# Top-k attention and two expert layers on one core: tiles regrouped over the last expert stages, conversions begun earlier, a pair's transposes put together

## The chip, the core and the metric

The kernel runs on one core of a Trainium2 chip. A core has TensorE (PE: matrix products, with a separate row, PEld, for its weight loads), VectorE (DVE), ScalarE (ACT), GpSimd (POOL) and SyncE (SP, which here only issues DMAs). Each engine takes its own instructions strictly in the order in which the program holds them. The metric is the device time of one execution in microseconds (us).

## The reference

Inputs: q, k, v of 2 batches x 8 heads x 576 rows x 64; 1152 tokens of 512 features leave the attention. What is computed, cut to its core:

```
scores = q k^T / 8;  kth = 32nd largest of each row;  keep scores >= kth
x   = softmax(kept scores) v                       # 1152 x 512
out = sum over 4 experts e of p[:, e] * (relu(x w1[e]) w2[e])      # hidden 1024
y   = max(out m1, out m2, out m3) m_out            # hidden 768
```

Everything is float32. The four weights of the last line (m1, m2, m3, m_out) arrive as 64-bit floats and are narrowed to 32 bits on the core.

## The kernel before

**Work items.** The 1152 tokens are 9 tiles of 128. The attention of one tile and one pair of heads is a "pair"; there are 36 pairs, numbered 0 to 35 in the order of `pairs`. For a pair and its two heads (j = 0, 1) the kernel computes scores (L419, L424, PE), copies them (L431, ACT), finds the 32 largest by four rounds of MAX8 and three of MATCH_REPLACE8 (L444, L446, DVE), masks and takes the exponential (L465 to L467 on ACT, or L458 on ACT and L472 on DVE), transposes the result (L490 and L495, PE; five transposes for j = 1 and the tail, four for j = 0), copies the transposes out (L493, L498, ACT), multiplies by v (L532, L535, PE, into `psv`), transposes the reciprocal of the sum (L518, `psr`), scales (L542, DVE) and splits the result into a high and a low part, `xh` (L555, ACT) and `xl` (L556, POOL).

**Slots.** `attention()` puts every step of pair n into a numbered slot, counted from 8n; dictionaries such as BOTH and LOOSE hold the offsets. `two(s, f, lag)` issues f in slot s and what f returns (mostly the copy out of PSUM) lag slots later. BOTH holds for pairs 8, 9, 10, 12, 13, 14; LOOSE for pairs 15 to 35; pair 11 has its own (THIRD), as have pairs 0 to 7. So in BOTH the transposes of j = 0 stand in slot 13, those of j = 1 and the tail in 14, their copies in 15 and 16; in LOOSE (trans=10, with the late mask of j = 0) the same. The product with v is in slot 17.

**Expert stages.** `STAGES` lists which tiles pass through which expert halves together. There are 9 stages, 0 to 8; even ones run the first 4 halves of the experts' hidden width, odd ones the last 4, so each tile is in one even and one odd stage. Before: [0], [0,1], [1,2], [2,3], [3,4], [4,5], [5], [6,7,8], [6,7,8]. A stage uses 16 weight blocks of 128x1024: 8 for the first layer ("a") and 8 for the second ("b"). In a stage of two or three tiles a product is done as three fast products of high and low parts (`product`, L681 to L683): 24 per first-layer block, with 128 columns per tile, and 6 of 512 columns per second-layer block and tile. Stages of one tile (`WHOLE`: 0 and 6) multiply plain float32 (L802: 8 per first-layer block, L843: 2 per second-layer block; each is recorded as two) and need no split weights. Elsewhere each block is split by `w_split_to`: a copy to the high part `whi` (L272, ACT) and the low part `wlo` (L278), in two halves on POOL, from stage LATE = 7 on every other block in one piece on DVE. `weight()` has blocks split up to W_AHEAD = 4 beyond the one in use.

**Who sets the order.** PE's expert work (`products`) is a generator. After each slot the main loop advances it until PE's estimated time has caught up with DVE's (`clock`), so expert matmuls fill PE between attention steps. A stage starts only when the attention of its newest tile is done.

**Conversions.** The 48 quarter blocks of the 64-bit weights go through `to_float32`: two ACT steps (L239, L240), three on DVE (L242, L244, L246), one on POOL (L249), and a DMA out (L254), spread over the slots. One starts every W_STEP = 2 slots from slot W_FROM = 306; their first loads (L223) are issued 6 slots before. The last attention steps are near slot 303.

Of the kernel before, what the change touches and what calls it, by code (L numbers as in the profile page):

```python
# [30 lines left out]
LATE = 7  # L31
ON_POOL = ((0, 1), (0, 1, 4))
W_AHEAD = 4
WIDE, W_FROM, W_STEP = 4, 306, 2
ON_ACT = (range(2, 36), (2, 5, 6, 8, 9, 10, 12, 13, 14))
STEEP = 2.0 ** 100
MASK_LATE = 2
# [3 lines left out]
TIGHT = dict(stag=3, new=1, scores=-7, at=(10, 11), guard=11, rec=11, spread=12, pv=12, turn=12, norm=13, split=13, last=14, lag=0, lag_s=1, sum=0, late=1)  # L41
SECOND = dict(TIGHT, norm=14, split=14, last=15)
THIRD = dict(stag=4, new=1, scores=-4, at=(11, 12), guard=12, rec=13, spread=13, pv=14, turn=14, norm=15, split=15, last=16, lag=0, lag_s=2, sum=0)
BOTH = dict(stag=4, new=1, scores=-4, at=(13, 14), pv=17, rec=15, lag=2, sum=0, late=1)
LOOSE = dict(stag=4, new=1, scores=-4, trans=10, pv=17, rec=15, lag=2, sum=0)

EARLY = 7

# [12 lines left out]
def kernel(  # L61
# [24 lines left out]
    NTILE = NT // P  # L86
# [7 lines left out]
    def batches(t):  # L94
        return (0, 1) if t == MIXED else (0 if t < MIXED else 1,)
# [2 lines left out]
    def place(t):  # L98
        return (t - 1) % RING

    STAGES = [[0]] + [[t - 1, t] for t in range(1, NTILE - 3)] + [[NTILE - 4]] + [[NTILE - 3, NTILE - 2, NTILE - 1]] * 2
    STAGES = [sorted(x, key=place) for x in STAGES]
    HALVES = [range(E) if not n % 2 else range(E, 2 * E) for n in range(len(STAGES))]
    WHOLE = [n for n, x in enumerate(STAGES) if len(x) == 1]
    FIRST_IN = {t: min(n for n, x in enumerate(STAGES) if t in x) for t in range(NTILE)}
    LAST_IN = {t: max(n for n, x in enumerate(STAGES) if t in x) for t in range(NTILE)}
    assert all(set(x for n in range(len(STAGES)) if t in STAGES[n] for x in HALVES[n]) == set(range(2 * E)) for t in range(NTILE))

# [3 lines left out]
    at = ctx.enter_context(tc.tile_pool(name="at", bufs=2))  # L112
# [445 lines left out]
    def attention():  # L558

        NP = len(pairs)  # L560
        prs = {}
        later, between = {}, {}

        def options(n):
            return TIGHT if n == HP - 1 else SECOND if n == 2 * HP - 1 else MIDDLE if n in (HP - 2, 2 * HP - 3, 2 * HP - 2) else FIRST if n < 2 * HP else THIRD if n == 3 * HP - 1 else BOTH if n in ON_ACT[1] else LOOSE

        def at_slot(s, f, *a):
            later.setdefault(s, []).append((f, a))


        first_use = {}
        for n, (c, hp, t) in enumerate(pairs):
            for b in batches(t):
                if ("v", b, hp) not in first_use:
                    first_use["v", b, hp] = n
                    at_slot(8 * n + (options(n)["pv"] - 7 if b and hp else 0), load_v, b, hp)
                if t >= FULL:
                    first_use.setdefault(("k", b, hp), n)
            if t >= FULL:
                first_use.setdefault(("q", c, hp), n)  # L580
            elif n:
                o = options(max(0, n - 2))
                at_slot(max(8 * n + options(n)["scores"] - LOAD_FULL, 8 * (n - 2) + o["scores"] + o["stag"] + 1), load_full, n)
        free = {"k": -99, "q": -99}
        for key, n in first_use.items():
            if key[0] == "v":
                continue
            s0 = 8 * n
            load, split = (load_k, split_k) if key[0] == "k" else (load_q, split_q)
            at = max(s0 + options(n)["scores"] - (SPLIT_K if key[0] == "k" else SPLIT_Q), free[key[0]] + 2)  # L590
            if key[0] == "k" and key[1] and key[2]:

                at = max(at, 8 * pairs.index((MIXED, key[2] - 1, MIXED)) + options(n)["scores"] + options(n)["stag"] + (1 if key[2] == HP - 1 else 4))
            at_slot(max(at - LOAD, free[key[0]] + 1), load, *key[1:])
            at_slot(at, split, *key[1:])
            free[key[0]] = at
        for n, (c, hp, t) in enumerate(pairs):
            s0 = 8 * n
            prs[n] = Pair(n)
            pr = prs[n]  # L600
            o = options(n)

            def two(s, f, *a, lag=o["lag"]):
                at_slot(s, lambda: at_slot(s + lag, f(*a)))
            for j in range(2):
                b0 = s0 + o["stag"] * j
                two(b0 + o["scores"], pr.scores, j, lag=o.get("lag_s", o["lag"]))
                for i in range(7):
                    if o["new"]:
                        later.setdefault(b0 + i, []).insert(0, (pr.topk, (j, i)))  # L610
                    else:
                        at_slot(b0 + i, pr.topk, j, i)
                at_slot(b0 + 2, pr.negate, j)
                at_slot(b0 + 5, pr.exp, j)
                late = o.get("late", MASK_LATE) * pr.on_act[j]
                two(b0 + 7 + late, pr.mask, j, lag=o["sum"] if n < EARLY else 3)
                two(s0 + o["at"][j] if "at" in o else b0 + o["trans"] + late + (late > 0), pr.trans_p, j)
            two(s0 + o["at"][1] if "at" in o else s0 + o["stag"] + o["trans"], pr.trans_p, 2)
            at_slot(s0 + o.get("guard", o["rec"] - 1), pr.guard)
            at_slot(s0 + o["rec"], pr.recip)  # L620
            at_slot(s0 + o.get("spread", o["rec"] + 1), pr.spread)
            at_slot(s0 + o["pv"], pr.pv)
            two(s0 + o.get("turn", o["rec"] + 2), pr.trans_r)
            end = max(o["pv"], o["rec"] + 2) + o["lag"]
            if "norm" in o:
                between.setdefault(s0 + o["norm"], []).append((pr.norm, ()))
            else:
                at_slot(s0 + end + 1, pr.norm)
            two(s0 + o.get("split", end + 2), pr.split_x)
        last = {}  # L630
        for n, p in enumerate(pairs):
            o = options(n)
            last[p[0:2]] = 8 * n + o.get("last", max(o["pv"], o["rec"] + 2) + 2 * o["lag"] + 2)
        for n in range(len(alone)):
            at_slot(ALONE_FROM + ALONE_STEP * n, load_alone, n + 1)
        end = max(last.values()) + 1
        s = min(later)
        while s <= end:
            todo = later.pop(s, [])
            i = 0  # L640
            while i < len(todo):
                f, a = todo[i]
                f(*a)
                todo[i + 1:i + 1] = between.pop(s, [])
                todo += later.pop(s, [])
                i += 1
            yield s, [c for c in last if last[c] + (READY if c[1] == HP - 2 else 0) == s]
            s += 1

        while narrowed[0] < WIDE * len(wide):  # L650
            clock["dve"] += PAUSE
            yield s, []
            s += 1


    lag = []
# [335 lines left out]
    for s, done in attention():  # L992
        if s == W_FROM - 6:
            for i in range(AHEAD_S):
                wide_load(i)
        if s >= W_FROM + W_STEP * conv and conv < WIDE * len(wide):
            converting.append(to_float32(conv))
            conv += 1
        for x in list(converting):
            if next(x, 0) == 0:  # L1000
                converting.remove(x)
        split_waiting()
        while any((x.c, x.hp) in done for x in waiting):
            assert advance()
            clock["goal"] = max(clock["goal"], clock["pe"])
            split_waiting()
        x_ready.update(done)
        clock["goal"] += (clock["dve"] - before) * SHARE[min(phase[0], len(SHARE) - 1)]
        before = clock["dve"]
        while clock["pe"] < clock["goal"]:  # L1010
            if not advance():
                clock["pe"] = clock["goal"]
                break
# [67 lines left out]
```

## Time and profile before

| | |
|---|---|
| median of 3 runs | 756.3 us (754.99 to 757.06) |
| the profiled execution | 755.31 us, its span 753.5 us |
| PE / DVE / ACT / POOL busy, share of the span | 97% / 80% / 66% / 61% |
| granted TensorE clock, mean | 0.998 |
| chain that ended last | PE 81%, ACT 8%, DVE 7% |

PE's busy share counts matmuls from start to a modelled end; they overlap, so the distance from one start to the next says what a matmul costs PE. What an engine waited for stands in brackets behind the instruction that waited. Pair 35's last attention step on PE (`psr`) begins at 446.04 us; before that, expert stages 0 to 6 and the attention share PE; after it come the rest of stage 6, stages 7 and 8, and the last layer.

### The profile page before, as it was taken

How to read it: one execution, taken by the hardware profiler on the slowest of the kernel's cores; microseconds unless marked ns; L12 is line 12 of the kernel's file. 1: busy time of each engine (PE TensorE's matmuls, PEld its weight loads, DVE VectorE, ACT ScalarE, POOL GpSimd, SP SyncE). 2: the span in 40 equal slices, each digit the busy share in tenths (PEclk: the TensorE clock that was granted, in tenths of full speed). 3: DMA queues.
4: the chain of work that ended last, by engine and by line, in shares of the span. 5: the costliest groups of instructions: out<-in, count | busy, mean ns of one | idle time of the engine just before them, and what ended most of it. 6: DMA issues, size and time to landing. Idle time of an engine off the chain costs nothing.

```text
span 753.5 us, 13557 instructions
## 1 busy us (share of the span) xinstructions
PE 728.9 (97%) x4678; PEld 643.6 (85%) x4678; DVE 604.8 (80%) x1160; ACT 495.1 (66%) x1127; POOL 457.7 (61%) x401
## 2 busy tenths in 40 slices
PE   6899998999999999999999999999999999999998
PEld 3586787878999998899988867999888899998996
DVE  6999987989999899999999958999999644233331
ACT  4668888889887887797796765666555533442531
POOL 2514777669979796787874316678677733442520
PEclk9999999999999999999999999999999999999999
DMA  7584554534646463534532769888688451443501
GB/s 221 180 269 153 160 179 156 151 100 134 212 129 196 124 195 110 181 120 149 158 121 90 251 216 352 248 263 284 219 266 267 142 187 69 154 168 104 190 1 43
DMA packets 56484, 130.14 MB, mean 173 GB/s; under 512 B 9760, under 2 KB 23328, under 8 KB 56416
## 3 DMA queue, kind: packets, MB, share of 16 engines
q1 hardware_dynamic: 48064, 120.69, 50.9%
q10 hardware_dynamic: 8352, 8.59, 3.2%
q8 instruction: 37, 0.61, 0.3%
q14 instruction: 31, 0.25, 0.1%
HBM read 120.60 MB, written 8.65 MB: 172 GB/s over the span
## 4 chain that ended last, share of the span: by engine, by line
PE 81%; ACT 8%; DVE 7%; issue 2%; POOL 1%; DMA 0%; ACTq 0%; POOLq 0%; DVEq 0%
PE ps L681 18%; PE ps L682 18%; PE ps L683 18%; PE psv L535 4%; PE pss L424 3%; DVE m L444 3%; PE psp L490 3%; DVE work L446 3%; ACT whi L272 2%; PE ps L843 2%; PE ps L802 2%; PE pso L682 2%; PE pso L681 2%; PE psa L766 2%; PE pso L683 2%
## 5 line engine op out<-in xcount | busy, mean ns | idle before, releaser
L278 POOL TENSOR_TENSOR wlo<-raw,whi 128x512 fp32r<-128x512 f32 x228 | 303.5, 1360 | 118.9 <-ACT whi L272 116.5
L272 ACT ACTIVATE whi<-raw 128x1024 fp32r<-128x1024 f32 x148 | 152.6, 1056 | 34.0 <-POOL narrow L249 16.4
L681 PE MATMUL ps<-xl,whi 128*128 128x256 f32 (+1 forms) x520 | 160.7, 309 | 0.1
L682 PE MATMUL ps<-xh,whi 128*128 128x256 f32 (+1 forms) x520 | 156.6, 301 | 0.0
L683 PE MATMUL ps<-xh,wlo 128*128 128x256 f32 (+1 forms) x520 | 156.5, 301 | 0.0
L444 DVE MAX8 m<-work 128x8 f32<-128x576 f32 x216 | 155.2, 745 | 0.1
L446 DVE MATCH_REPLACE8 work<-m,work 128x576 f32<-128x576 f32 x144 | 106.7, 741 | 0.0
L681 PEld LDWEIGHTS ps<-xl,whi 128*128 128x128 f32 x520 | 98.7, 190 | 1.5 <-POOL xl L556 0.3
L278 DVE TENSOR_TENSOR wlo<-raw,whi 128x1024 fp32r<-128x1024 f32 x34 | 53.3, 1567 | 57.3 <-ACT whi L272 45.1
L682 PEld LDWEIGHTS ps<-xh,whi 128*128 128x128 f32 x520 | 97.9, 188 | 1.2 <-issue 0.7
L683 PEld LDWEIGHTS ps<-xh,wlo 128*128 128x128 f32 x520 | 97.7, 188 | 0.0
L249 POOL TENSOR_TENSOR narrow<-narrow,raw 128x256 int32<-128x256 int32 x48 | 44.5, 927 | 40.1 <-DVE narrow L246 12.2
L681 PE MATMUL ps<-wlo,h 128*128 128x512 f32 x160 | 66.0, 413 | 0.6 <-POOL wlo L278 0.6
L683 PE MATMUL ps<-whi,h 128*128 128x512 f32 x160 | 63.2, 395 | 0.9 <-POOL h L818 0.9
L682 PE MATMUL ps<-whi,h 128*128 128x512 f32 x160 | 62.9, 393 | 0.0
L431 ACT ACTIVATE s<-pss 128x288 f32<-128x288 f32 x144 | 51.4, 401 | 12.6 <-PE pss L419 11.2
L444 DVE MAX8 m<-s 128x8 f32<-128x576 f32 x72 | 53.9, 748 | 4.5 <-ACT s L431 4.5
L446 DVE MATCH_REPLACE8 work<-m,s 128x576 f32<-128x576 f32 x72 | 53.4, 741 | 0.0
L493 ACT ACTIVATE pt<-psp 128x512 f32<-128x512 f32 x72 | 42.7, 594 | 16.2 <-PE psp L490 16.1
L683 PE MATMUL ps<-x2h,wlo 128*128 128x384 f32 x144 | 48.7, 338 | 0.0
L681 PE MATMUL ps<-x2l,whi 128*128 128x384 f32 x144 | 48.7, 338 | 0.0
L682 PE MATMUL ps<-x2h,whi 128*128 128x384 f32 x144 | 48.6, 337 | 0.0
(118 smaller groups left out, 1602.4 us busy)
## 6 DMA issues: line engine op xcount, KB each, us to landing
raw<-in_w_dram SPq DMA_DIRECT2D x112, 512.0 KB, 4.3
raw<-narrow SPq DMA_DIRECT2D x36, 512.0 KB, 3.9
whole<-in_w_dram SPq DMA_DIRECT2D x30, 512.0 KB, 5.5
raw<-in_m_dram SPq DMA_DIRECT2D x36, 256.0 KB, 4.8
narrow<-narrow ACTq DMA_DIRECT2D x48, 128.0 KB, 4.3
kraw<-in_k_dram SPq DMA_DIRECT2D x16, 288.0 KB, 4.3
qraw<-in_q_dram SPq DMA_DIRECT2D x48, 64.0 KB, 3.9
raw<-in_mo_dram SPq DMA_DIRECT2D x12, 256.0 KB, 4.1
```

What stands on the lines that cost most here:

```text
L249: nc.gpsimd.tensor_tensor(out=out.bitcast(I32), in0=out.bitcast(I32), in1=last, op=ALU.add)
L272: nc.scalar.activation(out=hi, in_=raw, func=AF.Copy)
L278: on.tensor_tensor(out=lo[:, x], in0=raw[:, x], in1=hi[:, x].bitcast(F32), op=ALU.subtract)
L424: nc.tensor.matmul(ps[:, 0:SH], lhsT=l, rhs=r, start=i == 0, stop=i == len(mm) - 1)
L431: nc.scalar.activation(out=s[:, h, :], in_=halves[h][:, 0:SH], func=AF.Copy)
L444: nc.vector.max(m[:, 8 * r:8 * r + 8], src)
L446: nc.vector.match_replace(out=self.w[j], in_to_replace=m[:, 8 * r:8 * r + 8], in_values=src, imm_value=NEG)
L493: return lambda: [nc.scalar.activation(out=d, in_=ps.rearrange("p (r n) -> p r n", r=NR), func=AF.Copy), self.did.add(("pt", part))]
L535: nc.tensor.matmul(ps[j * D:(j + 1) * D, cols], lhsT=vs[:, j * NR + r, :], rhs=self.pt[j][:, r, cols], start=False, stop=r == NR - 1)
L681: nc.tensor.matmul(ps, lhsT=lh, rhs=rl, start=first, stop=False)
L682: nc.tensor.matmul(ps, lhsT=lh, rhs=rh, start=False, stop=False)
L683: nc.tensor.matmul(ps, lhsT=ll, rhs=rh, start=False, stop=last)
```

## The change

Four settings and one argument:

```diff
-WIDE, W_FROM, W_STEP = 4, 306, 2
+WIDE, W_FROM, W_STEP = 4, 298, 2
-BOTH = dict(stag=4, new=1, scores=-4, at=(13, 14), pv=17, rec=15, lag=2, sum=0, late=1)
-LOOSE = dict(stag=4, new=1, scores=-4, trans=10, pv=17, rec=15, lag=2, sum=0)
+BOTH = dict(stag=4, new=1, scores=-4, at=(14, 14), pv=17, rec=15, lag=2, lag_t=1, sum=0, late=1)
+LOOSE = dict(stag=4, new=1, scores=-4, at=(14, 14), pv=17, rec=15, lag=2, sum=0)
-    STAGES = [[0]] + [[t - 1, t] for t in range(1, NTILE - 3)] + [[NTILE - 4]] + [[NTILE - 3, NTILE - 2, NTILE - 1]] * 2
+    STAGES = [[0]] + [[t - 1, t] for t in range(1, NTILE - 3)] + [[NTILE - 4, NTILE - 3], [NTILE - 3, NTILE - 2, NTILE - 1], [NTILE - 2, NTILE - 1]]
-                two(s0 + o["at"][j] if "at" in o else b0 + o["trans"] + late + (late > 0), pr.trans_p, j)
-            two(s0 + o["at"][1] if "at" in o else s0 + o["stag"] + o["trans"], pr.trans_p, 2)
+                two(s0 + o["at"][j] if "at" in o else b0 + o["trans"] + late + (late > 0), pr.trans_p, j, lag=o.get("lag_t", o["lag"]))
+            two(s0 + o["at"][1] if "at" in o else s0 + o["stag"] + o["trans"], pr.trans_p, 2, lag=o.get("lag_t", o["lag"]))
```

The stages after are [0], [0,1], ..., [4,5], [5,6], [6,7,8], [7,8]: stage 6 has two tiles and split weights instead of one tile and whole weights, stage 8 two tiles instead of three. In slots 298 to 305 four conversions now begin before the first of before did. All nine transposes of a pair from 8 on (but 11) stand in slot 14; their copies are in slot 15 (BOTH) or 16 (LOOSE).

ACT at pair 8, from the first copy of its transposes (`pt<-psp`) to the last; before:

```order
L493 ACTIVATE pt<-psp 128x512
L272 ACTIVATE whi<-raw 128x1024
L823 ACTIVATE h<-ps_1347 128x512
L513 ACTIVATE rb<-rr 128x128
L465 ACTIVATE s<-s,m_1193 128x576
L466 ACTIVATE nb<-m_1193,nb 128x1
L467 ACTIVATE p,rs<-s,nb 128x576
L493 ACTIVATE pt<-psp 128x512
L498 ACTIVATE pt_1372<-psp 128x128
```

The same place of ACT after:

```order
L493 ACTIVATE pt<-psp 128x512 x2
L498 ACTIVATE pt_1372<-psp 128x128
L272 ACTIVATE whi<-raw 128x1024
L823 ACTIVATE h<-ps_1341 128x512
L513 ACTIVATE rb<-rr 128x128
L465 ACTIVATE s<-s,m_1193 128x576
L466 ACTIVATE nb<-m_1193,nb 128x1
L467 ACTIVATE p,rs<-s,nb 128x576
```

The last two copies, for which the product with v waits, moved ahead of a weight copy, a relu and another head's mask and exponential (L465 to L467). In the same way they pass the mask and exponential at pairs 9, 12 and 13.

POOL where the attention ends (`xl` is the split of a pair's result, `narrow` a conversion, `wlo` a weight block's low part, `h` a hidden block's low part); before, the four `xl` are those of pairs 32 to 35:

```order
L278 TENSOR_TENSOR wlo<-raw,whi 128x512 x4
L818 TENSOR_TENSOR h<-raw,h 128x512
L556 TENSOR_TENSOR xl<-xt,xh 128x128 x4
L249 TENSOR_TENSOR narrow<-narrow,raw_6116 128x256
L249 TENSOR_TENSOR narrow<-narrow,raw_6118 128x256
L278 TENSOR_TENSOR wlo<-raw,whi 128x512 x2
```

POOL there after; the third row of `xl` is pair 35's:

```order
L278 TENSOR_TENSOR wlo<-raw,whi 128x512 x8
L556 TENSOR_TENSOR xl<-xt,xh 128x128 x2
L249 TENSOR_TENSOR narrow<-narrow,raw_6184 128x256
L249 TENSOR_TENSOR narrow<-narrow,raw_6186 128x256
L556 TENSOR_TENSOR xl<-xt,xh 128x128
L249 TENSOR_TENSOR narrow<-narrow,raw_6188 128x256
L278 TENSOR_TENSOR wlo<-raw,whi 128x512 x4
L818 TENSOR_TENSOR h<-raw,h 128x512
L249 TENSOR_TENSOR narrow<-narrow,raw_6190 128x256
L278 TENSOR_TENSOR wlo<-raw,whi 128x512 x2
L249 TENSOR_TENSOR narrow<-narrow,raw_6192 128x256
L278 TENSOR_TENSOR wlo<-raw,whi 128x512 x2
```

Ten of stage 6's 16 weight blocks are split ahead of the last three `xl`, the other six (two rows of `x2` are one block each, `x4` two) behind pair 35's, among conversions; the last two of the six follow two rows further on. Before, stage 6 had no splits, and nothing but `xl` and conversions stood here.

PE from the last attention step on; before:

```order
L518 MATMUL psr<-ident,rb 128x128
L802 MATMUL ps_6062<-xfull,whole 128x128 x4
L843 MATMUL ps_5978<-whole,hfull 128x512 x4
L802 MATMUL ps_6160<-xfull,whole 128x128 x8
L802 MATMUL ps_6186<-xfull,whole 128x128 x8
L843 MATMUL ps_6210<-whole,hfull 128x512 x4
```

After, it goes on from `psr` with two first-layer blocks of stage 6 (24 products of 256 columns each, into ps_6283 and ps_6325) and then a pair of second-layer blocks; the rows from the last product with v:

```order
L532 MATMUL psv<-pt_6209,v_last_110 128x128
L535 MATMUL psv<-pt,vt 64x128 x8
L518 MATMUL psr<-ident,rb 128x128
L681 MATMUL ps_6283<-xl,whi 128x256
L682 MATMUL ps_6283<-xh,whi 128x256
L683 MATMUL ps_6283<-xh,wlo 128x256
```

Half of stage 6 was behind the attention before, and about half is now, but as split products that need `wlo`.

## Rows read from the trace of the kernel before

**Rows 1.** Windows: length; busy us of PE, PEld, DVE, ACT, POOL; clock; DMA
```profile
100.00:140.00 40.00, 37.29 (x261) 33.07 (x260) 32.94 (x69) 35.57 (x81) 33.45 (x29) 0.96 0.58 179
200.00:440.00 240.00, 239.18 (x1844) 215.21 (x1843) 232.20 (x496) 189.14 (x460) 175.36 (x157) 1.00 0.51 159
460.00:580.00 120.00, 120.00 (x604) 107.84 (x603) 113.05 (x162) 72.95 (x144) 86.47 (x72) 1.00 0.83 265
```

**Rows 2.** Timeline, PE, fast products: start us, us, engine line op out<-in
```profile
401.61 0.28 PE L682 MATMUL ps<-xh,whi 128*128 128x256 f32 x1
...
404.20 0.28 PE L683 MATMUL ps<-xh,wlo 128*128 128x256 f32 x1
...
457.72 0.34 PE L682 MATMUL ps<-xh,whi 128*128 128x384 f32 x1
...
464.82 0.34 PE L681 MATMUL ps<-xl,whi 128*128 128x384 f32 x1
...
499.94 0.40 PE L681 MATMUL ps<-wlo,hh 128*128 128x512 f32 x1
...
502.50 0.40 PE L683 MATMUL ps<-whi,hl 128*128 128x512 f32 x1
```

**Rows 3.** Timeline, PE, whole products of stage 6
```profile
447.10 3.60 PE L843 MATMUL ps<-whole,hfull 128*128 128x512 f32 x8
450.54 3.73 PE L802 MATMUL ps<-xfull,whole 128*128 128x128 f32 x32
454.11 3.60 PE L843 MATMUL ps<-whole,hfull 128*128 128x512 f32 x8
```

**Rows 4.** Timeline, PE, products with v that waited [idle before <-releaser]
```profile
119.17 0.76 PE L532 MATMUL psv<-pt,v_last 128*128 128x128 f32 x2 [2.12 <-ACT pt L498]
...
168.83 0.49 PE L532 MATMUL psv<-pt,v_last 128*128 128x128 f32 x2 [0.82 <-ACT pt L498]
...
181.43 0.49 PE L532 MATMUL psv<-pt,v_last 128*128 128x128 f32 x2 [1.77 <-ACT pt L498]
```

**Rows 5.** Timeline, ACT, from pair 8's mask step to its last copy
```profile
116.59 0.79 ACT L465 ACTIVATE s<-s,m 128x576 f32<-128x576 f32 x1
...
118.85 0.27 ACT L498 ACTIVATE pt<-psp 128x128 f32<-128x128 f32 x1
```

**Rows 6.** Timeline, PE, around a set of nine transposes
```profile
425.38 0.48 PE L681 MATMUL ps<-wlo,h 128*128 128x512 f32 x1
425.70 0.40 PE L682 MATMUL ps<-whi,h 128*128 128x512 f32 x1
```

**Rows 7.** Timeline, end of the attention on PE, POOL and ACT
```profile
446.04 0.33 PE L518 MATMUL psr<-ident,rb 128*128 128x128 f32 x1
...
447.50 0.46 POOL L556 TENSOR_TENSOR xl<-xt,xh 128x128 fp32r<-128x128 f32 x1 [4.02 <-ACT xh L555]
...
449.80 1.08 ACT L272 ACTIVATE whi<-raw 128x1024 fp32r<-128x1024 f32 x1
```

**Rows 8.** Groups by line, POOL, 100:440, 440:470, 470:600: xcount | busy, mean ns
```profile
L278 POOL TENSOR_TENSOR wlo<-raw,whi 128x512 fp32r<-128x512 f32 x152 | 193.6, 1305 | 34.5 <-ACT whi L272 34.3
...
L278 POOL TENSOR_TENSOR wlo<-raw,whi 128x512 fp32r<-128x512 f32 x6 | 8.8, 1491 | 1.1 <-issue 1.1
L249 POOL TENSOR_TENSOR narrow<-narrow,raw 128x256 int32<-128x256 int32 x7 | 5.4, 769 | 6.0 <-ACT raw L240 1.2 <-ACT narrow L239 1.2 <-DVE narrow L246 1.2
...
L278 POOL TENSOR_TENSOR wlo<-raw,whi 128x512 fp32r<-128x512 f32 x30 | 46.4, 1568 | 3.8 <-ACT whi L272 3.6
```

**Rows 9.** Groups by line, DVE, 470:600: the three conversion steps
```profile
L242 DVE SCALAR_TENSOR_TENSOR raw<-narrow,raw 128x256 f32<-128x256 f32 x41 | 28.9, 705 | 0.0
L244 DVE TENSOR_SCALAR narrow<-raw 128x256 uint32<-128x256 uint32 x41 | 28.9, 704 | 1.4
...
L246 DVE SCALAR_TENSOR_TENSOR narrow<-raw,narrow 128x256 uint32<-128x256 uint32 x41 | 24.4, 595 | 1.4
```

**Rows 10.** Tile narrow, DVE, first conversion step: xcount: ns min/median/max
```profile
L242 DVE SCALAR_TENSOR_TENSOR raw<-narrow,raw x48: 414/424/1521, 447.8 to 592.2; 128x256 f32<-128x256 f32 x48
```

## The prediction

> **What bounds the kernel now.** I read the windows first. Between 200 and 440 us PE is busy for 239.18 of 240 us and between 460 and 580 for all of it [rows 1]. DVE comes next with 232.20 and 113.05. A busy PE need not be at its peak, so I went to the timeline and took the distance between starts: 22 steps from 401.61 to 404.20 make 0.1177 us for a product of 256 columns, 41 steps from 457.72 to 464.82 make 0.1732 for 384, and 11 from 499.94 to 502.50 make 0.2327 for 512 [rows 2]. They follow each other without holes, so in these stretches the time is the sum of PE's work, and a change is worth the PE work it takes out plus the waits it takes out or puts in. PE's own waits are the third view. After 100 us they are few; the largest are products with v that wait for the copy of their transposes [rows 4].
>
> **The regrouped stages.** Stage 6 with one tile has 128 recorded products of 128 columns, of which 32 take from 450.54 to 454.11, 0.1116 each, and 32 of 512, of which 8 take from 447.10 to 450.54, 0.430 each [rows 3]: 14.3 + 13.8 = 28.1 us. With two tiles it has 8 blocks x 24 = 192 products of 256 columns and 8 x 6 x 2 = 96 of 512: 192 x 0.1177 + 96 x 0.2327 = 22.6 + 22.3 = 44.9 us [rows 2]. That is 16.8 more. Stage 8 loses a tile: 192 x (0.1732 - 0.1177) + 48 x 0.2327 = 10.7 + 11.2 = 21.9 us less. Together PE has 5.1 us less to do, all of it on the path. DMA moves the same 16 blocks. ACT gets 16 copies of 1.08 [rows 7], which lie in its idle 51 us of the window 200 to 440 [rows 1] and behind it. The hidden blocks' low parts move between stages and roughly cancel.
>
> **The new wait.** The 16 splits on POOL are the price. Ten are issued while the attention still shares PE, where POOL is idle for 65 of 240 us [rows 1]: I cost them at nothing. The other six stand behind the split of pair 35's result and three conversions, and PE comes to them without any attention in between. Take the start of the last `psr` (446.04) as zero. PE has 0.25 left of it and then, per two blocks, 5.6 us: first-layer blocks, second-layer pair, first-layer blocks, second-layer pair, done at 22.7 if nothing waits. On POOL the split of the last result ends 1.9 after zero (447.50 + 0.46), and the weight copy on ACT, behind conversions as in before, starts at 3.8 (449.80) and ends at 4.8 [rows 7]. From there POOL runs block 1, block 2, a hidden block's low part, conversion, block 3, conversion, block 4, conversion, block 5, block 6. What is queued behind matters: PE's use of block 2 needs the hidden block too, and all later PE work stands behind PE's wait.
>
> The rows give three prices for half a split: 1.305 beside top-k, 1.491 at the first conversions, 1.568 among conversions; a conversion is 0.769 [rows 8]; a hidden block's low part is an operation of the size of half a split, and I take 1.3 for it. With 1.491: block 2 is done at 4.8 + 4 x 1.491 = 10.8, the hidden block at 12.1, where PE wanted it at 7.25: 4.8 us late. Block 5 then ends at 23.3 and block 6 at 26.3; PE waits for the halves of both and ends the second pair at 29.8 in place of 22.7. That is 7.1 us lost. With 1.305 the same sum gives 4.9, with 1.568 it gives 8.0. I take 7.1, since the six blocks fall where the row of 1.491 was taken, at the first conversions. The lower bound is nothing, if POOL or ACT gets ahead of my order.
>
> DVE's conversion steps share something with POOL: the first one takes 414 ns at best and 1521 at worst [rows 10], and the difference is a little less than half a split beside top-k. The Trainium skill ("SBUF — State Buffer", Who interferes with whom) says that a DVE instruction with two SBUF inputs and a GpSimd instruction that reads SBUF exclude each other for a whole instruction. The trace agrees in size. By that rule five conversions with two such steps of 0.41 each would add 4.1 to the price of 4.9, 9.0 in all instead of 7.1. The rows that I use already hold a part of this, so I stay with 7.1.
>
> **The transposes.** At pairs 8, 12 and 13 the last copies stand behind another head's mask and exponential; at pair 8 this begins at 116.59 and the copy ends at 119.12 [rows 5], and PE waits 2.12, 0.82 and 1.77 us for them [rows 4]. In the new order the copies stand ahead of those steps, and at pair 8 of a weight copy and a relu as well, which is at least as much as the waits. So 4.7 us go. What is late next: the steps that were passed, by about a copy each, and they have slots to spare. Bounds: 4.7, and nothing, if PE waits elsewhere for what DVE has not done. I take 4.7, because from 200 to 440 PE is the full engine and DVE has 8 us to spare [rows 1]: time won before 200 can be kept. Putting the two sets of transposes together takes away 20 interruptions of the products; the first product after one costs 0.32 (425.38 to 425.70) instead of 0.23 [rows 6]. That is 1.8 at most; I take 0, since the nine still change their PSUM bank in the middle.
>
> **The earlier conversions.** Their DVE steps fall where attention has no more DVE work. Their loads are moved on SP ahead of the weight loads of blocks 4 to 6, and each waits for a score buffer or an earlier conversion; block 4 is not split before 15.8 after zero in the sum above, so that there is room for its load. Three conversions stand ahead of the first of the six splits, which is in the 4.8 above. I cost the rest at nothing; they end no later than before.
>
> **Sum.** -5.1 (PE work) - 4.7 (waits gone) + 7.1 (POOL's splits) = -2.7. The profiled execution took 755.3 with a span of 753.5, so 752.6 is the forecast. The median of the runs shown is 756.3, 1.0 above that execution; a repeat of it may read up to that much higher.
>
> **The rivals.** *POOL keeps up.* Between 200 and 440 POOL splits every block that PE uses, and PE has less than 1 us without work [rows 1]. If the six splits cost nothing, -9.8: 745.5. Against it: there PE also had attention to do between blocks, here it has not.
>
> *DVE and POOL hold each other up*, the slower side. A conversion takes 0.705 + 0.704 + 0.595 = 2.0 us of DVE [rows 9]. From 460 to 580 about 38 of them (41 in 130 us) are 76 of DVE's 113 us; the other 37 are for 29 weight blocks (4.16 us of PE each with three tiles), 1.3 a block. In a last stage of two tiles a block lasts 2.8 us: 16 x 1.3 = 20.8, and some 15 conversions in it are 30, together 50.8 against 44.9 of PE. If nothing absorbs that, 5.9 us are lost there, and the splits cost 8.0 instead of 7.1: -2.7 + 5.9 + 0.9 = +4.1, 759.4. It decides once DVE has no idle time in the last paired stage. For it: DVE is 94% busy there already. Against it: PE took no wait at 94%, four blocks are split ahead, and PE's wait in stage 6 gives DVE time to catch up. The lock that the Trainium skill states (the page above) would work in the same direction.
>
> *The waits come back.* If the order around pairs 8 to 13 is really held by DVE, PE waits elsewhere: -5.1 + 7.1 = +2.0, 757.3. For it: DVE is the next fullest engine [rows 1]. Against it: around the longest of them, from 100 to 140 us, DVE is busy for 32.94 of 40 us only [rows 1].
>
> **How the numbers follow.** The forecast 0.40, with 749.5 to 755.5 as its own range (the splits 4.9 to 8.0, the waits 3 to 4.7); POOL keeps up 0.25; DVE and POOL 0.22; the waits come back 0.13. A measurement of this kernel can tell about 0.3%, 2.3 us, from no change. Faster by more than that (below 753.0): all of the second case and 0.6 of the first, 0.49. Within: the rest of the first less a little, and most of the last, 0.26. Slower (above 757.6): 0.25. The range for 8 in 10 is 746 to 759.5; it reaches both outer cases but not the 1.8 of the transposes below nor the full rule of the lock above.
>
> **What would show it.** Right: no wait of a `psv` near 119, 168 and 181 us; L802 and L843 gone; about 5 us less of PE's starts summed up; and, within 30 us behind the last `psr`, waits of PE for `wlo` or `h` of POOL of about 7 us. The second case shows none of these; the third shows waits for `wlo` of DVE in stage 8 with DVE at full share; the fourth shows new waits of PE before 200 us. I am wrong altogether if the clock falls below the 1.00 of now [rows 1] while PE waits, or if conversions end so late that the last layer waits for them.

## The result and the profile after

The changed kernel takes 765.2 us (median of 5 runs, 765.12 to 766.03), the kernel before, timed beside it, 757.1 (754.99 to 758.87): ratio 1.012, 95% interval 1.0101 to 1.014. It is slower, by some 1.2%. The forecast was 752.6 with a range of 746 to 759.5. The profiled execution took 765.73 with a span of 763.9, 10.4 more than before's 753.5.

Windows of the kernel after, columns as in [rows 1], which the first three rows answer; the last runs from the last `psr` to the first product of the last layer:

```profile
100.00:140.00 40.00, 38.95 (x280) 34.62 (x279) 35.55 (x76) 37.73 (x88) 35.59 (x31) 1.00 0.63 187
200.00:440.00 240.00, 238.20 (x1841) 215.49 (x1839) 231.08 (x492) 191.62 (x459) 193.37 (x169) 1.00 0.49 149
460.00:580.00 120.00, 115.61 (x627) 101.81 (x626) 117.02 (x145) 72.27 (x138) 97.24 (x78) 0.99 0.81 261
446.00:606.00 160.00, 149.10 (x821) 129.02 (x817) 153.67 (x198) 96.36 (x184) 128.09 (x104) 0.98 0.77 249
```

The last window in the kernel before:

```profile
446.00:606.00 160.00, 160.00 (x808) 141.03 (x807) 141.70 (x207) 94.45 (x188) 110.07 (x92) 1.00 0.76 247
```

PE no longer fills the stretch behind the attention: 149.10 of 160 us against 160.00, while DVE is busy for 12.0 and POOL for 18.0 us more. Before 140 us PE is fuller than it was. The timeline of PE after (start, us, engine, line), with the `psr` of pairs 8 and 13, the last `psr`, some products of stage 6, and the first product of the last layer:

```profile
118.79 0.33 PE L518 MATMUL psr<-ident,rb 128*128 128x128 f32 x1
...
177.20 0.33 PE L518 MATMUL psr<-ident,rb 128*128 128x128 f32 x1
...
446.81 0.33 PE L518 MATMUL psr<-ident,rb 128*128 128x128 f32 x1
...
459.19 0.39 PE L682 MATMUL ps<-whi,h 128*128 128x512 f32 x1
...
460.34 0.63 PE L683 MATMUL ps<-whi,h 128*128 128x512 f32 x1
460.76 0.63 PE L681 MATMUL ps<-wlo,h 128*128 128x512 f32 x1
...
606.29 0.45 PE L681 MATMUL ps<-x2l,whi 128*128 128x384 f32 x1 [1.31 <-DVE x2l L908]
```

In before these four `psr` and last-layer marks stand at 121.77, 182.88, 446.04 [rows 7] and 596.03. So after is 3.0 us ahead at pair 8, 5.7 ahead at pair 13, 0.8 behind at the last `psr` (by count PE has done 3.6 us more of its work by then, so it is still 2.8 us ahead in work) and 10.3 behind at the last layer; from there before takes 157.5 and after 157.6 to the end. What makes it slower than before lies between the last two marks. There PE has 288 products of 256 columns, 192 of 384 and 312 of 512: 288 x 0.1177 + 192 x 0.1732 + 312 x 0.2327 [rows 2] = 139.8, 141.2 with the transposes. It takes 159.5: 18.3 us are lost. In before the same stretch took 150.0 without a hole. PE's waits in it (total, times, longest):

```profile
PE ps L683 <- POOL h L818: 4.1, 3, 2.0
PE ps L683 <- POOL hl L818: 2.3, 2, 1.8
PE ps L681 <- POOL wlo L278: 1.7, 4, 0.5
PE psv L532 <- ACT pt L498: 1.5, 1, 1.5
PE ps L681 <- ACT h L817: 1.4, 1, 1.4
PE ps L681 <- DVE x2l L908: 1.3, 1, 1.3
PE ps L681 <- DVE wlo L278: 0.2, 1, 0.2
```

All but the `psv` wait (just ahead of the last `psr`) belong to it: 11.0 us, spread over stages 6, 7 and 8 and the start of the last layer. With what PE needs to get going again the distances between starts are 13.0 above the steps of [rows 2] at these places. Behind two of them, from 459.9 and from 599.8 us on, the clock is at the lower of its two levels (1.2 of 2.4 GHz): 512 columns take 0.42 (460.34 to 460.76) instead of 0.2327 for eight products, 1.6 us each time. The other 2 us are in holes too small to follow. By place, waits and slow clock cost 5.4 us in stage 6 and 10.7 in stages 7 and 8 and ahead of the last layer. The windows around the two slow places show the clock (last but two) below 1.00:

```profile
450.00:470.00 20.00, 16.83 (x98) 14.06 (x97) 18.38 (x20) 13.47 (x23) 19.58 (x18) 0.91 0.82 261
590.00:610.00 20.00, 16.37 (x74) 13.19 (x73) 18.03 (x27) 11.39 (x21) 15.20 (x13) 0.91 0.61 208
```

Groups by line, DVE, 446 to 606 us (count | busy, mean ns | idle before), kernel before, then after:

```profile
L242 DVE SCALAR_TENSOR_TENSOR raw<-narrow,raw 128x256 f32<-128x256 f32 x48 | 33.1, 689 | 0.7 <-ACT narrow L239 0.7
L244 DVE TENSOR_SCALAR narrow<-raw 128x256 uint32<-128x256 uint32 x48 | 32.7, 681 | 1.6
L278 DVE TENSOR_TENSOR wlo<-raw,whi 128x1024 fp32r<-128x1024 f32 x19 | 30.5, 1607 | 10.7 <-ACT whi L272 9.8 <-DMA narrow<-narrow 0.9
L246 DVE SCALAR_TENSOR_TENSOR narrow<-raw,narrow 128x256 uint32<-128x256 uint32 x48 | 28.4, 591 | 1.6
```

```profile
L246 DVE SCALAR_TENSOR_TENSOR narrow<-raw,narrow 128x256 uint32<-128x256 uint32 x48 | 40.3, 839 | 1.6
L244 DVE TENSOR_SCALAR narrow<-raw 128x256 uint32<-128x256 uint32 x48 | 35.0, 730 | 1.6
L242 DVE SCALAR_TENSOR_TENSOR raw<-narrow,raw 128x256 f32<-128x256 f32 x48 | 35.0, 729 | 3.1 <-ACT narrow L239 2.5 <-issue 0.6
L278 DVE TENSOR_TENSOR wlo<-raw,whi 128x1024 fp32r<-128x1024 f32 x18 | 29.7, 1651 | 1.1 <-POOL narrow L249 1.1
...
L825 DVE SCALAR_TENSOR_TENSOR hl<-ps,hh 128x384 fp32r<-128x384 f32 x12 | 6.1, 544 | 0.0
```

The same 48 conversions take 94.2 us of DVE before and 110.3 after: 1.96 us each has become 2.30, and the idle time ahead of the splits has gone from 10.7 to 1.1 us. The same instructions got longer. POOL has more splits in the stretch, and each takes no longer than before (1.46 us against 1.53). On POOL, before and after:

```profile
L278 POOL TENSOR_TENSOR wlo<-raw,whi 128x512 fp32r<-128x512 f32 x39 | 59.0, 1534 | 7.7 <-ACT whi L272 6.5 <-issue 1.1
```

```profile
L278 POOL TENSOR_TENSOR wlo<-raw,whi 128x512 fp32r<-128x512 f32 x49 | 70.2, 1455 | 1.0 <-ACT whi L272 0.6
...
L818 POOL TENSOR_TENSOR h<-raw,h 128x512 fp32r<-128x512 f32 x4 | 5.7, 1425 | 0.0
```

### The profile page after: what moved, and what is told of

Its sections match the earlier page's. It is cut to its first block, busy times and chain, and to the rows that moved or that the text cites. A ratio compares the mean times of both kernels' runs of the same rounds, so it can differ in the third digit from the quotient of the medians.

```text
span 763.9 us, 13775 instructions
## 1 busy us (share of the span) xinstructions
PE 729.3 (95%) x4758; PEld 644.0 (84%) x4758; DVE 625.9 (82%) x1161; ACT 508.2 (67%) x1137; POOL 503.3 (66%) x433
## 5 line engine op out<-in xcount | busy, mean ns | idle before, releaser
L278 POOL TENSOR_TENSOR wlo<-raw,whi 128x512 fp32r<-128x512 f32 x258 | 341.1, 1351 | 116.6 <-ACT whi L272 112.5
L272 ACT ACTIVATE whi<-raw 128x1024 fp32r<-128x1024 f32 x164 | 169.5, 1056 | 47.2 <-POOL narrow L249 19.1
L681 PE MATMUL ps<-xl,whi 128*128 128x256 f32 (+1 forms) x584 | 173.5, 297 | 0.4 <-POOL xl L556 0.4
L682 PE MATMUL ps<-xh,whi 128*128 128x256 f32 (+1 forms) x584 | 170.7, 292 | 0.0
L683 PE MATMUL ps<-xh,wlo 128*128 128x256 f32 (+1 forms) x584 | 170.7, 292 | 0.0
L681 PE MATMUL ps<-wlo,h 128*128 128x512 f32 x224 | 92.9, 415 | 4.0 <-POOL wlo L278 2.2
L683 PE MATMUL ps<-whi,h 128*128 128x512 f32 x224 | 89.7, 400 | 5.4 <-POOL h L818 5.4
L682 PE MATMUL ps<-whi,h 128*128 128x512 f32 x224 | 89.2, 398 | 0.0
L249 POOL TENSOR_TENSOR narrow<-narrow,raw 128x256 int32<-128x256 int32 x48 | 50.4, 1050 | 32.8 <-DVE narrow L246 10.7
L683 PEld LDWEIGHTS ps<-whi,h 128*128 128x128 f32 x224 | 42.9, 192 | 17.1 <-POOL h L818 7.5
L681 PEld LDWEIGHTS ps<-wlo,h 128*128 128x128 f32 x224 | 43.6, 195 | 14.9 <-POOL wlo L278 5.6
L948 DVE TENSOR_TENSOR tm<-ps,tm 128x384 f32<-128x384 f32 x36 | 19.9, 555 | 35.2 <-PE ps L683 33.3
```

What stands on the lines that cost most here:

```text
L249: nc.gpsimd.tensor_tensor(out=out.bitcast(I32), in0=out.bitcast(I32), in1=last, op=ALU.add)
L272: nc.scalar.activation(out=hi, in_=raw, func=AF.Copy)
L278: on.tensor_tensor(out=lo[:, x], in0=raw[:, x], in1=hi[:, x].bitcast(F32), op=ALU.subtract)
L681: nc.tensor.matmul(ps, lhsT=lh, rhs=rl, start=first, stop=False)
L682: nc.tensor.matmul(ps, lhsT=lh, rhs=rh, start=False, stop=False)
L683: nc.tensor.matmul(ps, lhsT=ll, rhs=rh, start=False, stop=last)
```

## The experiments

Each kernel ran beside the kernel before on the same chip; a time is a median in us, a ratio is against the kernel before, with its 95% interval. Three theories came to be told apart. A: DVE has more instructions than PE's shortened time there. B: the six POOL splits behind the last `psr` are the cause, and later waits are what they hand on. C: DVE and POOL lengthen each other's work, so the two together are the bound. Before the runs the earlier conversions were a suspect too, called C in the first expectations.

**The parts of the change.** Four kernels take parts of the change back, in this manner:

```
e1_trans, e4_trans_from:        STAGES as in before
e2_stages:                      BOTH, LOOSE and trans_p's lag as in before
e1, e2, e3_stages_trans:        W_FROM = 306 as in before
```

e1_trans, only the transposes and copies changed:

> The transposes and their copies as changed; stages and the slot of the first conversion as before. All theories: the three waits of the product with v near 119, 168 and 181 us go, 4.7 us, and up to 1 comes back elsewhere: ratio 0.994 to 0.996, about 752.5 against 756.5. If the early gain were lost again before the end (the waits come back), the ratio would be 1.000.

Measured: 752.3 us, ratio 0.995 (0.9926 to 0.9973).

e4_trans_from, transposes and earlier conversions:

> Transposes as changed and conversions from slot 298; stages as before. Theory A (DVE is the bound from the end of the attention to the end of the conversions, because the new stages leave it less PE time per conversion): with the old stages DVE has slack, so the same as with the transposes alone, within 1.5 us. Theory C (the earlier conversions themselves are the harm): slower than the transposes alone by 5 us or more.

Measured: 753.8, ratio 0.996 (0.9937 to 0.9983).

e2_stages, only the stages:

> The new stages alone; transposes, copies and conversions as before. Theory A: the time of the new stages with the transposes plus 4 us, 769 to 773, so over 12 us slower than before. Theory B: 764 to 767. Theory C: 755 to 760.

Measured: 772.5, ratio 1.0217 (1.0175 to 1.0259).

e3_stages_trans, all but the earlier conversions:

> The whole change but conversions from slot 306 as before. Theory A: DVE has the same work in less time, so as slow as the change or slower: 765 to 769, with PE's waits moved from stage 6 to stages 7 and 8. Theory B (stage 6's six late splits on POOL are the cause, and the waits in stages 7 and 8 are what they hand on): less POOL work beside the splits, 760 to 763. Theory C: at or below the time before, 750 to 757.

Measured: 769.1, ratio 1.0158 (1.0121 to 1.0195). So the new transposes are worth 3.8 us (2.0 to 5.6), the new stages cost some 17 (e3 against e1, e2 against before), and the earlier conversions are no harm: after is 3.8 below e3 by the medians and 2.9 by the ratios, whose intervals overlap, and e4 against e1 shows nothing either. The loss comes with the new stages.

**Less DVE work.** e5_fewer_dve:

```
-        nc.vector.tensor_scalar(out=t, in0=high, scalar1=3, ...)
-        nc.vector.scalar_tensor_tensor(out=t, in0=high, scalar=0xC0000000, ...)
```

> The changed kernel with two of the three DVE steps of every conversion left out (L244 and L246, so part of the narrowing isn't computed); the order of all else is the same. It takes about 64 x 1.5 us of DVE work away and touches no split on POOL. Theory A (from the last psr to the last conversion DVE has more work than PE's time there, so PE waits wherever DVE is late): the 12 us of PE's waits between 510 and 610 us go, and the slow clock behind them; 749 to 754. Theory B (the six POOL splits behind the last psr are the cause, and the later waits are what they hand on): POOL is as late as before, so 759 to 764.

Measured: 753.2, ratio 0.9962 (0.9941 to 0.9983), as A said. PE's waits from 440 to 620 us, and behind them, from 446 to 606 us, the one conversion step that is left on DVE and POOL's splits (here code lines from L246 on are numbered two lower than in after):

```profile
PE ps L681 <- POOL h L816: 1.9, 1, 1.9
PE ps L679 <- DVE x2l L906: 1.5, 1, 1.5
PE psv L530 <- ACT pt L496: 1.4, 1, 1.4
PE ps L679 <- POOL wlo L276: 0.6, 2, 0.5
```

```profile
L242 DVE SCALAR_TENSOR_TENSOR raw<-narrow,raw 128x256 f32<-128x256 f32 x48 | 40.8, 864 | 17.0 <-POOL narrow L247 9.2 <-ACT narrow L239 7.3 <-issue 0.4
...
L276 POOL TENSOR_TENSOR wlo<-raw,whi 128x512 fp32r<-128x512 f32 x54 | 78.0, 1469 | 16.4 <-ACT whi L270 12.5 <-DMA raw<-in_m_dram 2.8 <-POOL narrow L247 1.0
```

The waits of stages 7 and 8 are gone though POOL has every split that it had and is busy for 132.95 of 160 us, more than in after. B falls as the whole cause, and so does POOL's own load. It doesn't tell A from C: the steps left out may be steps that POOL lengthens. But the step that stayed got longer, from 0.73 to 0.86 us, beside 54 half splits on POOL in place of 49 and with DVE busy for 94.30 us in place of 153.67: its length doesn't come from DVE's load.

**The six splits.** e9_no_six makes the low part of these six on ACT, e13_hi_twice not at all, e8_six_shared gives three of them to DVE:

```
e9   if -6 <= late < 0: nc.scalar.activation(out=lo, in_=raw, func=AF.Copy)
e13  lo = hi if -6 <= late < 0 else wp.tile(...)
e8   on = nc.vector if late >= -6 and late % 2 else nc.gpsimd
```

> The changed kernel, in which the low parts of the last six blocks of stage 6 are made by a copy on ACT instead of two half splits on POOL (the subtraction of these six is left out). POOL loses 6 x 2.7 = 16 us behind the last psr, DVE keeps its instructions. Theory A: the waits of stage 6 go (5.4 us), and DVE's conversions beside them shorten by some us, but stages 7 and 8 are held by DVE still: 757 to 761. Theory B: all of it goes: 748 to 753.

Measured: 763.7, ratio 1.0102 (1.0073 to 1.013), in neither range. The experiment brought a bound of its own, as the window (PE, PEld, DVE, ACT, POOL) shows:

```profile
450.00:470.00 20.00, 18.02 (x113) 15.67 (x112) 11.28 (x23) 19.46 (x30) 7.45 (x10) 1.00 0.92 324
```

ACT is full with the copies and DVE stands idle for 8.7 of 20 us, 4.6 of them for want of ACT's conversion step (L239). It settles nothing; e13 does what e9 was to do.

> The changed kernel, in which the last six blocks of stage 6 have no split at all: their products take the high part twice (their low parts are left out), so PE, ACT and DVE have the same instructions and POOL 16 us less. Theory A: stage 6's waits go and come back later, 760 to 764. Theory B (the six splits are the whole cause): 748 to 753. Theory C: the waits of stage 6 (5.4 us) go, and the 10 conversions beside them shorten by 0.4 to 0.6 us each: 753 to 759.

Measured: 757.6, ratio 1.0028 (1.0009 to 1.0047), in C's range. The conversions fall from 2.30 to 2.12 us each.

> The changed kernel with three of those six splits on DVE (one instruction of 1.6 us each) instead of POOL; everything is computed. Theory A: stage 6 waits less, but DVE has 4.8 us more to do before its last conversion, and the end is set there: 763 to 768. Theory B: half of the cause is gone: 756 to 760.

Measured: 765.2, ratio 1.011 (1.0079 to 1.0141), as A said: stage 6 waits less and the last layer comes no sooner (605.9 us against 606.3). In its profile the stretch from the last `psr` to the last layer is 2.4 us shorter (157.1), but that `psr` stands 2.0 us later (448.76), for which no run gives a reason. Theory C would have this kernel faster than after, with six halves fewer on POOL; by its time it isn't.

**Splits of stages 7 and 8 moved between DVE and POOL.** One line, with a third, two thirds or all of them on DVE instead of half (it rules the last layer's splits as well), and in e14 stage 6's six besides:

```
e10  on = nc.vector if late >= 0 and late % 3 == 1 else nc.gpsimd
e11  on = nc.vector if late >= 0 and late % 3 else nc.gpsimd
e12  on = nc.vector if late >= 0 else nc.gpsimd
e14  on = nc.vector if late >= -6 else nc.gpsimd
```

> The changed kernel with every third instead of every second split of stages 7 and 8 on DVE: DVE has 5 or 6 splits of 1.6 us less, POOL as many of 2.7 us more; everything is computed. Theory A: DVE is 8 to 9 us earlier, less what its conversions lose to POOL: 758 to 763. Theory B: POOL is later still: 766 to 772.

Measured: 771.4, ratio 1.0205 (1.0176 to 1.0234). A is wrong in sign: DVE had fewer instructions, and the kernel became slower. B's range holds it, but B had fallen with e5. DVE's groups, 446 to 606 us, show why:

```profile
L246 DVE SCALAR_TENSOR_TENSOR narrow<-raw,narrow 128x256 uint32<-128x256 uint32 x47 | 45.4, 966 | 1.6
L242 DVE SCALAR_TENSOR_TENSOR raw<-narrow,raw 128x256 f32<-128x256 f32 x46 | 38.5, 838 | 1.8 <-ACT narrow L239 0.7 <-POOL narrow L249 0.6 <-issue 0.4
L244 DVE TENSOR_SCALAR narrow<-raw 128x256 uint32<-128x256 uint32 x46 | 37.5, 816 | 1.6
L278 DVE TENSOR_TENSOR wlo<-raw,whi 128x1024 fp32r<-128x1024 f32 x12 | 18.9, 1574 | 0.7 <-ACT whi L272 0.7
```

Six splits fewer took 10.8 us off in this stretch, and a conversion went from 2.30 to 2.62 us, which makes 15 more for 48. From this came theory C.

> The changed kernel with two of three splits of stages 7 and 8 on DVE instead of every second: DVE has 5 splits of 1.65 us more, POOL as many of 2.9 us less; everything is computed. Theory A (the number of DVE's instructions is the bound): 8 us later, 770 to 774. Theory C (DVE and POOL hold each other up, so that each split on POOL lengthens the conversions beside it, and the time is set by both together; a third instead of a half on DVE cost 6 us): the other way round, 758 to 764.

Measured: 762.6, ratio 1.0095 (1.0081 to 1.0109), in C's range and 7 below A's.

> The changed kernel with all splits of stages 7 and 8 on DVE: DVE has 16 splits of 1.65 us more, POOL 16 of 2.9 us less; everything is computed. Theory A: 26 us more of DVE's work, some of it after the last conversion: 780 to 790. Theory C: the some 38 conversions of these stages get back to 1.96 us or below from about 2.3, so that at least 13 us come back: 764 to 776; if they fall to 1.5, 755 to 763.

Measured: 755.5, ratio 1.0 (0.9983 to 1.0017). In C's range and 24 us below A's.

> The changed kernel with all splits of stages 7 and 8 and the last six of stage 6 on DVE; everything is computed. Theory C (DVE and POOL lengthen each other's work, and a split is cheaper for the two together on DVE): the waits of stage 6 go as well, of which the kernel with all splits of stages 7 and 8 on DVE still has 3.2 us and a slower clock: 750 to 754. If DVE has by now too much of its own: 755 to 760.

Measured: 751.5, ratio 0.9947 (0.9928 to 0.9965): the same stages are 20 us faster than in e10, with 48 splits on DVE in this stretch where e10 has 12, and faster than the kernel before. From e1 and e15 it can't be told apart. DVE's groups and one of POOL in it, 446 to 606 us:

```profile
L278 DVE TENSOR_TENSOR wlo<-raw,whi 128x1024 fp32r<-128x1024 f32 x48 | 61.7, 1308 | 4.8 <-ACT whi L272 4.0 <-issue 0.7
L242 DVE SCALAR_TENSOR_TENSOR raw<-narrow,raw 128x256 f32<-128x256 f32 x47 | 30.7, 654 | 0.0
L246 DVE SCALAR_TENSOR_TENSOR narrow<-raw,narrow 128x256 uint32<-128x256 uint32 x48 | 21.5, 448 | 1.6
L244 DVE TENSOR_SCALAR narrow<-raw 128x256 uint32<-128x256 uint32 x48 | 20.4, 425 | 1.6
...
L825 DVE SCALAR_TENSOR_TENSOR hl<-ps,hh 128x384 fp32r<-128x384 f32 x12 | 6.1, 548 | 0.0
```

```profile
L818 POOL TENSOR_TENSOR h<-raw,h 128x512 fp32r<-128x512 f32 x4 | 8.0, 1997 | 2.0 <-ACT h L817 2.0
```

The splits, 1.65 us each in after, take 1.31, and every conversion step on DVE is shorter; on POOL the low parts and the conversion step (L249) got longer.

**The control.** e15_trans_all_dve is e1 with e12's line:

> The old stages and conversions with the new transposes (752.3 us before) and all splits of stages 7 and 8 on DVE; everything is computed. Theory C: there PE is the bound and DVE and POOL have time to spare, so the same shift that takes 10 us from the changed kernel takes nothing here: 750.5 to 754. If it gains there too (below 749), the 10 us are not due to what the new stages leave to DVE and POOL.

Measured: 752.1, ratio 0.9956 (0.9941 to 0.9972), against 0.995 of e1: nothing. Its window:

```profile
446.00:606.00 160.00, 160.00 (x814) 142.49 (x813) 133.91 (x224) 92.13 (x180) 55.37 (x52) 1.00 0.78 255
```

POOL has half the work, DVE 6.6 us less than in e1 with 20 splits more, and PE is as full as before. The shift is worth something only where the new stages leave PE less to do. All of it in one table, for 446 to 606 us of each profile:

| kernel | splits on DVE / halves on POOL | the three steps, us | DVE, POOL busy | PE busy of 160 | time, us (ratio) |
|---|---|---|---|---|---|
| before | 19 / 39 | 1.96 | 141.7, 110.1 | 160.0 | 757.1 (1) |
| e1 old stages | 19 / 40 | 2.00 | 140.5, 111.6 | 160.0 | 752.3 (0.995) |
| e15 old stages | 39 / 0 | 1.44 | 133.9, 55.4 | 160.0 | 752.1 (0.996) |
| e10 new stages | 12 / 58 | 2.62 | 153.7, 136.3 | 146.6 | 771.4 (1.021) |
| after | 18 / 49 | 2.30 | 153.7, 128.1 | 149.1 | 765.2 (1.012) |
| e8 | 21 / 43 | 2.19 | 153.3, 122.4 | 147.7 | 765.2 (1.011) |
| e11 | 26 / 38 | 2.08 | 153.3, 113.7 | 150.4 | 762.6 (1.010) |
| e12 | 40 / 12 | 1.73 | 150.9, 81.1 | 154.1 | 755.5 (1.000) |
| e14 | 48 / 0 | 1.53 | 148.7, 66.7 | 157.6 | 751.5 (0.995) |

With the new stages each column falls or rises in one order, but for e8, where PE's share is below that of after and the time the same; the steps of a conversion do so in all of them. A plainer rival is left in part: 8.1 of PE's 11.0 us of waits in after name POOL, and e10 to e14 also change how many splits stand ahead of these instructions in POOL's order. e5 speaks against POOL's load alone; how much of the gain from e10 to e14 comes of shorter steps on DVE and how much of a shorter queue on POOL no run separates. Conversion steps alone, tile `narrow` on DVE (ns min/median/max), one in after and then two in e14:

```profile
L244 DVE TENSOR_SCALAR narrow<-raw x48: 293/726/1821, 446.1 to 604.4; 128x256 uint32<-128x256 uint32 x48
```

```profile
L244 DVE TENSOR_SCALAR narrow<-raw x48: 293/295/761, 445.9 to 588.7; 128x256 uint32<-128x256 uint32 x48
L246 DVE SCALAR_TENSOR_TENSOR narrow<-raw,narrow x48: 424/426/1394, 446.2 to 589.0; 128x256 uint32<-128x256 uint32 x48
```

## Why the prediction was wrong

**The step that failed** is the sum's missing term: behind stage 6 the forecast gave DVE and POOL no cost at all. Waits and slow clock cost 10.7 us there. The third rival had the mechanism, the side and the place, at 759.4 with a chance of 0.22; what happened is about twice its size: it stood 6.8 above the forecast, and the profiled execution (765.7) stands 13.1 above it. Its own sign came in part: DVE was full (19.6 of every 20 us from 500 to 600), but PE waited for `wlo` of DVE for 0.2 us only, and mostly for POOL. It took 2.0 us per conversion from [rows 9] and held it fixed, and priced the exchange with POOL at 0.9 us, as a dearer split in stage 6. The runs show that the 2.0 was itself made by POOL: 1.44 where POOL has no split, 2.62 where it has 58 halves. With more splits on POOL in less PE time it became 2.30, 16 us over 48 conversions. The spread 414 to 1521 ns of [rows 10] was read as a matter of stage 6 alone. The prediction says that its range reaches both outer cases; its lower end, 746, lies above the second rival's 745.5. No rival stood near 765.

**PE's work.** The 5.1 us are right by count (5.2 with the transposes), but they were not gained: 141.2 us of work took 159.5. In e14 it takes 144.0. Even so e14 begins the last layer only 1.6 us before e15, which has the old stages (590.63 against 592.25), and their times, 751.5 and 752.1, can't be told apart: that the new stages are worth their 5 us once POOL is relieved isn't shown.

**The six splits.** Predicted 7.1 us lost in stage 6, 4.8 at the first pair of blocks and the rest at the second; the waits there are 3.8, all at the first pair, and the slow clock, which the sum didn't have, adds 1.6. So 5.4 lies near 7.1 partly by luck. Taking the six away gives 7 to 8 us (e13: 757.6 against 765.2, ratios 1.003 and 1.012), as the conversions beside them shorten too: the term missed what the splits do later.

**The waits of `psv`** went as said: predicted 4.7 us, measured 3.8 (e1, spans 753.5 and 749.7; 2.0 to 5.6 by its interval). The waits at 119, 168 and 181 us are gone; of those of `psv` from 60 to 440 us 2.1 us are left of 6.1; these are all waits of a `psv` or `psp` from 60 to 440 us after that exceed half a microsecond in total:

```profile
PE psv L532 <- ACT pt L498: 2.1, 3, 1.0
...
PE psp L495 <- ACT raw L816: 1.3, 2, 0.8
```

So the fourth rival is wrong, and the second (POOL keeps up) falls with the waits for `wlo` and `h`.

**The earlier conversions**, costed at nothing, did no harm; the 3 to 4 us by which after lies below e3 are inside the intervals.

**What would show it.** Both signs named for being wrong altogether came: the clock at 0.91 between 450 and 470 and between 590 and 610 us while PE waits, and a last layer that waits 1.3 us for `x2l` of DVE, which stands right behind the steps of the last conversion (602.81 to 605.02).

**The lock.** The Trainium skill ("SBUF — State Buffer", Who interferes with whom) says that a DVE instruction with two SBUF inputs, or one in a two-port mode, and a GpSimd instruction that reads SBUF exclude each other for the whole instruction, and that a DVE instruction with at most one SBUF input outside those modes is left alone. The runs agree: the split on DVE (two inputs) went from 1.65 to 1.31 us and the step L244 from a median of 726 to 295 ns, while L825, which has one input in PSUM, took 544 to 551 ns in every profile. L244 has one SBUF input, so it fits the rule only in such a mode; no row names the mode (at its shortest it takes 293 ns for the 256 columns for which L246 takes 424). The prediction weighed this rule in numbers for stage 6 only and then stayed with the smaller number. What the two engines share wasn't isolated by a run of its own; that DVE's durations fall as POOL's splits are taken away is what is shown.

## What to carry to other kernels

A duration from the profile of before holds only while its neighbours stay: ask of each mean whether its minimum is far below (293 against 681 ns for L244 before), and what sets the difference. Where one engine's instructions get longer beside another's, count the two together; work given to the one with idle time can slow the fuller one, and here moving the splits onto the fuller engine made the kernel 20 us faster (e10 to e14). When PE's work in a stage is cut, make the sum of what the other engines must do in the shortened stage first.

## What was not expected of the hardware

Giving DVE more to do lowered its busy time: 153.7 of 160 us with 12 splits and 46 conversions (e10), 148.7 with 48 splits and 47 conversions (e14). The other way the effect is smaller: POOL's conversion step grew from 0.90 to 1.11 us between the same two, and POOL has time for that:

```profile
L249 POOL TENSOR_TENSOR narrow<-narrow,raw 128x256 int32<-128x256 int32 x47 | 42.4, 903 | 22.0 <-issue 8.3 <-DVE narrow L246 5.3 <-DMA narrow<-narrow 2.9
```

```profile
L249 POOL TENSOR_TENSOR narrow<-narrow,raw 128x256 int32<-128x256 int32 x48 | 53.2, 1109 | 77.3 <-DVE narrow L246 23.7 <-ACT whi L272 14.0 <-ACT raw L240 9.4
```

PE ran at the lower clock for eight products each time behind four waits (3.2 us in all, the longest 2.0) and behind two (1.4 and 0.9 us). In e14, where these waits are shorter, no stretch of 20 us between 440 and 620 shows a clock below 1.00.
